# Strassen over the last 192 rows of a down projection as two 96-row halves

## The chip, the cores and the metric

The kernel runs on one core of one Trainium2 chip. The metric is device time in microseconds (us) of that core for one execution. "Span" is the part of it that a profile records; it is about 2 us shorter than the time (254.3 against 256.17 us in the profiled run of the kernel before). I give the ratios with their 95% intervals.

## The reference, cut to what matters

The block is a layer norm with modulation, a spectral filter, a second layer norm with modulation, and a SwiGLU feed-forward part. Only the last part is changed.

```python
# x: (1, 2048, 640), w_gate and w_up: (640, 1728), w_down: (1728, 640), all bf16
h = _layernorm(x, axis=-1) * (1 + cb) + sb
x = x + gb * ((silu(h @ w_gate) * (h @ w_up)) @ w_down)
```

The inner width is 1728 = 12 x 128 + 192. The 192 rows left over are the subject.

## The kernel before

The 2048 tokens are taken in five chunks of 2, 4, 4, 4 and 2 token tiles (128 tokens each). In each chunk TensorE first makes gate and up, and then the down projection. Chunk 0 is done plainly. In chunks 1 to 4 both parts use Strassen's scheme (Winograd's variant) with seven products for eight. In the down projection two token tiles are a "pair"; the halves of the inner width are six blocks of 128 rows each, and the halves of the output are 320 columns. The left-hand sums S1 to S4 are made by VectorE for each pair, the sums T1 to T4 of the weights once. Block 12 (128 rows) and block 13 (64 rows) stay outside the scheme and are multiplied plainly, partly in a folded form (`S12`, `W13`).

```python
def down_pair(ATc, t, j, nxt):                     # a pair of token tiles
    X, Y, Z = (psum[:, next_banks(1), 0:320] for _ in range(3))
    ...
    mm(Z, r13[0:64], Wd_sb[0:64, 13, 0:320], True)           # two 64-row matmuls
    mm(Y, r13[64:128], Wd_sb[64:128, 13, 320:640], True)
    prod(X, A11, B11, True, True)
    nc.scalar.copy(cps_[0], X)
    nc.gpsimd.tensor_tensor(xa[:, 0:320], xa[:, 0:320], cps_[0], ALU.add)
    for k in range(3):
        mm(Z, A12[:, k], B21[:, k])
    prod(Y, S1, T1)
    nxt(0)                                         # VectorE: a sum of the next pair
    mm(Y, ATc[:, 12, tb:tb + 128], w12(1), stop=True)
    nc.scalar.copy(cps_[1], Y)
    prod(X, S2, T2, stop=True)
    nxt(1)
    nc.scalar.copy(cps_[2], X)
    nc.gpsimd.tensor_tensor(xb[:, 320:640], xb[:, 320:640], cps_[1], ALU.add)
    prod(Y, S4, B22)
    nxt(3)
    nc.gpsimd.tensor_tensor(xa[:, 320:640], xa[:, 320:640], cps_[2], ALU.add)
    prod(X, S3, T3, stop=True)
    nc.scalar.copy(cps_[3], X)
    nxt(2)
    ...                                            # blocks 12 and 13, the rest of Z
    prod(X, A22, T4, stop=True)                    # accumulates on the same bank X
    out_store(t, Z, 0)                             # VectorE adds x1, then a store
    out_store(t + 1, X, 0)
```

Gate and up of block 13 share one matmul. Its result lies with gate in partitions 0 to 63 and up in 64 to 127, so it is brought together by four evacuations and two transfers:

```python
def gu13(ci, ATc):
    ...
    nc.scalar.activation(m13[0:64], gv[0:64, 1], ACT.Silu)
    nc.vector.tensor_copy(m13[64:128], gv[64:128, 0])
    nc.scalar.activation(f13[0:64], gv[0:64, 0], ACT.Silu)
    nc.vector.tensor_copy(f13[64:128], gv[64:128, 1])
    nc.sync.dma_start(b13[0:64], m13[64:128])
    nc.sync.dma_start(b13[64:128], m13[0:64])
```

Between gate/up and the pairs of chunk 1 stand the statistics of the second layer norm for token tiles 10 to 15:

```python
if ci == 1:
    ln2_var(10, 6)        # VectorE, 3 small operations
    ln2_pow(10, 6)        # GpSimd, the power -1/2
    ln2_nb(10, 6)         # VectorE, the bias -mean * rstd
...
g21b, g22b = (rL.cut(1024 * i, [512]) for i in range(2))      # gate activations, bytes 0 to 2048 of rL
cps_ = [rL.cut((2560, 10496, 0, 1280)[i], [320], F32) for i in range(4)]   # cps_[2] is at byte 0 of rL
```

## Time and profile before

The median was 256.27 us (256.12 to 256.96, 3 runs). The span of the profile is 254.3 us.

The profile page of the kernel before, first lines: busy time of each engine with its share of the span, and the granted TensorE clock by slices.

```profile
PE 244.9 (96%) x2520; PEld 199.5 (78%) x2520; DVE 208.0 (82%) x521; ACT 163.7 (64%) x305; POOL 73.6 (29%) x117
...
PEclk9999999999999999999999999999999999999999
```

PE is TensorE, DVE VectorE, ACT ScalarE, POOL GpSimd. TensorE is busy for 96% at the full clock. VectorE with 82% is next, and I take it for a likely second limit wherever its work is bunched.

The view of waits of TensorE, kernel before, from 85 to 250 us (engine, tile, line, what it waited for, then total, number, longest):

```profile
PE psum L933 <- DVE rX L1037: 0.8, 1, 0.8
PE psum L1058 <- ACT rH L1090: 0.2, 1, 0.2
```

So in the whole feed-forward part TensorE waited about 1 us. The longer of the two waits is in the last pair. The timeline of TensorE shows it, and shows the start of a pair of chunk 1 (start, duration, engine, line, operation, tiles, shape, count, and in brackets the idle time before):

```profile
134.03 0.27 PE L1058 MATMUL psum<-rW,rH 128*128 128x256 bf16 x1
134.24 1.64 PE L933 MATMUL psum<-rA,rX 64*128 64x320 bf16 x11
...
246.42 0.31 PE L933 MATMUL psum<-rA,rX 128*128 128x320 bf16 x1 [0.78 <-DVE rX L1037]
```

The starts of the single matmuls show what the grouped line hides. The first 64-row matmul starts 205 ns after the last gate/up matmul, where 109 are usual there. The second starts 4 ns after the first. The next full one starts 239 ns later, then comes 146, then 136 ns each. The trace records the two as 64*128, the matmuls around them as 128*128. Together the starts are about 0.2 us a pair longer than the usual ones (205 less 109, 4 + 239 less 136, and 146 less 136). "Drain" is my name for this extra time; the trace doesn't show what TensorE does in it.

### The profile page before, as it was taken

The numbers are of one execution on the slowest core, as the hardware profiler recorded it, in microseconds if no ns is written. First come the engines' busy times: TensorE is split into PE (matmuls) and PEld (weight loads), VectorE is DVE, ScalarE is ACT, GpSimd is POOL, SyncE is SP. The second block draws the span as 40 slices with busy tenths as digits, with TensorE's granted clock in tenths as the row PEclk, the third lists the DMA queues.
The fourth block names the chain that finished last, engine by engine and source line by source line (L and its number), as shares of the span: only waits on it lengthen the run. The fifth ranks groups of instructions, "written<-read, shape, count | busy, mean of one in ns | idle before, by whom it ended". The sixth has DMA issues, their size and how long they took to land.

```text
span 254.3 us, 6501 instructions
## 1 busy us (share of the span) xinstructions
PE 244.9 (96%) x2520; PEld 199.5 (78%) x2520; DVE 208.0 (82%) x521; ACT 163.7 (64%) x305; POOL 73.6 (29%) x117
## 2 busy tenths in 40 slices
PE   8899987999999999999999999999999999999984
PEld 3788856999788887788877678886668886679953
DVE  2898888888888897979997995879985788994793
ACT  3778656988778698578863477673356766235730
POOL 4387756764021805000004600001430000440021
PEclk9999999999999999999999999999999999999999
DMA  7989999999999899710005120002411000212001
GB/s 222 389 278 336 306 394 190 270 275 390 309 332 281 221 257 156 153 36 0 3 0 106 39 70 8 3 3 52 92 40 35 3 0 4 52 52 59 4 0 52
DMA packets 46588, 34.78 MB, mean 137 GB/s; under 512 B 22111, under 2 KB 43486, under 8 KB 46174
## 3 DMA queue, kind: packets, MB, share of 16 engines
q1 hardware_dynamic: 44892, 30.36, 43.2%
q0 software_dynamic: 1376, 3.93, 6.6%
q8 instruction: 19, 0.31, 0.5%
q10 hardware_dynamic: 290, 0.08, 0.1%
q14 instruction: 11, 0.09, 0.1%
HBM read 26.80 MB, written 4.72 MB: 124 GB/s over the span
## 4 chain that ended last, share of the span: by engine, by line
PE 69%; DVE 5%; ACT 4%; DMA 3%; SPq 2%; issue 1%; DVEq 0%; ACTq 0%
PE psum L1058 29%; PE psum L933 17%; PE psum L1031 8%; DMA rM<-in_w_mod_dram 3%; PE psum L645 3%; SPq L504 2%; PE psum L803 2%; PE psum L580 2%; PE psum L806 2%; PE psum L912 1%; PE psum L551 1%; DVE rA L898 1%; PE psum L601 1%; PE psum L1010 1%; PE psum L650 1%
## 5 line engine op out<-in xcount | busy, mean ns | idle before, releaser
L1058 PEld LDWEIGHTS <-rW 128*128 128x128 bf16 (+1 forms) x528 | 47.0, 98 | 5.9 <-issue 0.6
L949 POOL TENSOR_TENSOR rM<-rM,rL 128x320 f32<-128x320 f32 x7 | 6.2, 885 | 86.4 <-ACT rL L948 86.4
L1058 PE MATMUL psum<-rE,rW 128*128 128x256 f16 (+1 forms) x192 | 27.7, 259 | 0.2 <-ACT rH L1090 0.2
L1058 PE MATMUL psum<-rW 128*128 128x256 bf16 (+1 forms) x240 | 27.1, 259 | 0.0
L1058 PE MATMUL psum<-rY,rW 128*128 128x256 bf16 (+1 forms) x96 | 24.0, 259 | 0.0
L573 DVE TENSOR_TENSOR rM<-psum,rW 128x384 bf16<-128x384 f32 (+2 forms) x42 | 20.4, 542 | 3.7 <-PE psum L551 3.4
L933 PEld LDWEIGHTS <-rX 128*128 128x128 bf16 (+1 forms) x181 | 16.1, 97 | 9.2 <-issue 1.6
L1031 PE MATMUL psum<-rW 128*128 128x256 bf16 (+1 forms) x170 | 23.2, 291 | 0.0
L933 PEld LDWEIGHTS <-rE 128*128 128x128 f16 x168 | 16.4, 98 | 6.5 <-DVE rE L884 0.2
L933 PE MATMUL psum<-rE 128*128 128x320 f16 x126 | 20.4, 299 | 0.0
L933 PE MATMUL psum<-rA,rX 128*128 128x320 bf16 (+1 forms) x119 | 19.5, 301 | 0.8 <-DVE rX L1037 0.8
L1031 PEld LDWEIGHTS <-rW 128*128 128x128 bf16 x170 | 16.6, 98 | 3.8
L1058 PEld LDWEIGHTS <-rE 128*128 128x128 f16 x192 | 17.4, 98 | 2.3
L1108 DVE TENSOR_TENSOR rX<-rH,rL 128x512 bf16<-128x512 bf16 x21 | 8.9, 425 | 11.7 <-ACT rL L1106 11.5
L736 POOL TENSOR_TENSOR rstd<-rstd,mhalf 128x4 f32<-128x4 f32 (+2 forms) x4 | 4.7, 1187 | 44.8 <-DVE rstd L732 44.8
L1098 DVE TENSOR_TENSOR rX<-psum,rX 128x512 f32<-128x512 f32 x21 | 14.4, 688 | 3.2 <-ACT rX L1097 2.9
L1097 ACT COPY rX<-psum 128x512 f32<-128x512 f32 x21 | 12.3, 587 | 7.2 <-PE psum L1058 7.1
L1094 DVE TENSOR_TENSOR rH<-psum,rW 128x512 bf16<-128x512 f32 x21 | 14.5, 690 | 2.4 <-PE psum L1058 0.6
L1090 ACT COPY rH<-psum 128x512 f32<-128x512 f32 x21 | 12.2, 581 | 6.4 <-PE psum L1058 5.7
L1084 ACT COPY rW<-psum 128x512 f32<-128x512 f32 x21 | 12.3, 586 | 5.8 <-PE psum L1058 5.8
L390 DVE SCALAR_TENSOR_TENSOR rE<-rE,mv,psum 128x648 bf16<-128x648 f32 (+1 forms) x17 | 14.1, 841 | 2.0 <-PE psum L323 1.6
L1058 PE MATMUL psum<-rW,rE 128*128 128x256 bf16 (+1 forms) x96 | 15.1, 259 | 0.0
(203 smaller groups left out, 665.5 us busy)
## 6 DMA issues: line engine op xcount, KB each, us to landing
out_dram<-rA SPq DMA_DIRECT2D x31, 80.0 KB, 1.6
rM<-in_w_mod_dram SPq DMA_DIRECT2D x3, 800.0 KB, 9.2
rA<-in_B_w_down_dram SPq DMA_DIRECT2D x1, 2080.0 KB, 12.8
rX<-in_A_x_dram SPq DMA_DIRECT2D x3, 640.0 KB, 7.2
rM<-in_w_mod_dram SPq DMA_DIRECT2D x1, 1600.0 KB, 8.0
rY<-in_B_w_gate_dram POOLq DMA_DIRECT2D x2, 768.0 KB, 6.9
rW<-in_B_w_gate_dram SPq DMA_DIRECT2D x2, 640.0 KB, 7.0
rW<-in_B_w_up_dram SPq DMA_DIRECT2D x2, 640.0 KB, 8.0
```

Of the source, the lines that this page charges most:

```text
L390: nc.vector.scalar_tensor_tensor(Zv[:, h], Cv[:, h], mv[:, t, 0:1], zps[:, h], ALU.mult, ALU.subtract)
L573: nc.vector.tensor_tensor(PP[:, :, hl], xv[:, :, hl], in1, ALU.mult)
L645: nc.tensor.matmul(vps[:, r, :], lhsT=Em[:, v, 4 * t + r, :], rhs=Htab[:, t, v, :], start=(v == 0), stop=(v == 1))
L933: nc.tensor.matmul(o, lhsT=lhsT, rhs=rhs, start=start, stop=stop, skip_group_check=True)
L1031: nc.tensor.matmul(gu[u], lhsT=Wgu[:, u, c5, ff * 128:(ff + 1) * 128], rhs=h2T[:, :, c5, :], start=(c5 == 0), stop=(c5 == NC5 - 1))
L1058: nc.tensor.matmul(o[:, f], lhsT=w, rhs=b, start=(start and f == 0 and i == 0), stop=(stop and f == F - 1 and i == len(ops) - 1), skip_gro ...
L1084: nc.scalar.copy(c0, X)
L1090: nc.scalar.copy(c2, X)
L1094: nc.vector.tensor_tensor(c11, Z, c0, ALU.add)
L1097: nc.scalar.copy(c3, X)
L1098: nc.vector.tensor_tensor(c22, Y, c3, ALU.add)
L1108: nc.vector.tensor_tensor(ato, v4(c11), v4(g21), ALU.mult)
```

## The change

The intent is to take the last 192 rows into Strassen's scheme. They become two halves of 96 rows, so that each of the seven products has seven matmuls, the last of 96 rows, and nothing is left outside. Blocks 12 and 13 are stored as rows 1536 to 1632 and (in another order) 1632 to 1728. The transfers between partitions go: VectorE multiplies the up half in partitions 64 to 127 by the activated gate half in partitions 0 to 63. A fourth PSUM bank W takes the last product, so bank X is added to the input by GpSimd, as the fourth addition of a pair.

```diff
-        mm(Z, r13[0:64], Wd_sb[0:64, 13, 0:320], True)
-        mm(Y, r13[64:128], Wd_sb[64:128, 13, 320:640], True)
-        prod(X, A11, B11, True, True)
+        W = psum[:, next_banks(1), 0:320]
+        last = t + 2 == NT
+        prod(X, half(0, ta), wd(0, 0), True, True)       # half(), s7(): 6 x 128 rows and 96 rows
 ...
-        prod(X, S3, T3, stop=True)
-        nc.scalar.copy(cps_[3], X)
+        prod(X, s7(2), t7(2), stop=True)
 ...
+            nc.scalar.copy(cps_[3], X)
+            nc.gpsimd.tensor_tensor(xb[:, 0:320], xb[:, 0:320], cps_[3], ALU.add)
+            out_store(t + 1, cps_[3], 1)
+            prod(W, half(1, tb), t7(3), True, True)
+            out_store(t + 1, W, 0)
 ...  # gate and up of the 64-row block
-        nc.sync.dma_start(b13[0:64], m13[64:128])
-        nc.sync.dma_start(b13[64:128], m13[0:64])
+        nc.scalar.activation(sg13, g13[0:64], ACT.Silu)
+        return lambda: nc.vector.tensor_tensor(ATc[0:64, 13, :], g13[64:128], sg13, ALU.mult)
 ...  # block 12 of gate and up: 96 rows, and 32 rows that go to block 13
+                    nc.vector.tensor_tensor(ATc[0:RK, 12, :], gu[1][0:RK], sg[0:RK, 0:N], ALU.mult)
+        half.rest = lambda: nc.vector.tensor_tensor(ATc[64:RK, 13, :], gu[1][RK:P], sg[RK:P, 0:N], ALU.mult)
 ...  # VectorE order at the end of gate/up of a chunk of four tiles
-            run(2)
-            step(5, nG - 1)
-            step(7, nG - 1)
+            later[:0] = [half.rest, q1, q2]               # q1 to q4: the 96-row sums of the first pair
+            later.extend([q3, q4, lambda: step(8, nG - 1), lambda: step(7, nG - 1)])
+            step(5, nG - 1, True)
 ...  # in the first pair: sums of the second
-                    if n == 4:
+                    if n == 4 and i < 4:
                         a_sum(ATc, 1, i)
+                        a_sum7(ATc, 1, i)
```

The full diff holds more moves: the product Z runs in one piece, the last pair gets its own order, block 13 of chunk 0 moves in front of the last spectral tile, and some squares of the second layer norm come earlier.

The rest product and the four 96-row sums of the first pair now stand before the statistics of chunk 1 in VectorE's order, and the last product of the group (`step(7)`) now comes after them.

More of the change, by code (lines that the diff above doesn't have):

```diff
@@ L29 @@
 IDLE = (3, 6, 1, 2)
+RK = 96
 _NPBF = ml_dtypes.bfloat16
@@ L698, in adaln_block_kernel @@
         nc.vector.tensor_tensor(RI[:, 0], RI[:, 0], ga_bc[:], ALU.mult)
-    nc.sync.dma_start(Wd_sb[:, 0:13, :], B_w_down[0:1664, :].rearrange("(fc fp) d -> fp fc d", fp=P))
-    for h in range(2):
-        nc.sync.dma_start(Wd_sb[64 * h:64 * h + 64, 13, :], B_w_down[1664:1728, :])
+    nc.sync.dma_start(Wd_sb[:, 0:12, :], B_w_down[0:1536, :].rearrange("(fc fp) d -> fp fc d", fp=P))
+    nc.sync.dma_start(Wd_sb[0:RK, 12, :], B_w_down[1536:1632, :])
+    nc.sync.dma_start(Wd_sb[0:64, 13, :], B_w_down[1664:1728, :])
+    nc.sync.dma_start(Wd_sb[64:RK, 13, :], B_w_down[1632:1664, :])
     Wgu = rW.cut(0, [2, NC5, 13 * 128])
@@ L790, in wd_fold @@
     def wd_fold(f2):
-        nc.vector.tensor_tensor(Wd_sb[:, f2, :], Wd_sb[:, f2, :], gb_bc[:], ALU.mult)
-    if True:
-        VTs = {0: s1er(0), 1: s1er(1)}
-        nc.vector.tensor_copy(gb_bc[:, 0:320], mod_bc(3, 0, 7))
-        for t in range(NT):
-            if t and t + 1 < NT:
-                s1em(t + 1)
-                VTs[t + 1] = s1er(t + 1)
-            VT = VTs.pop(t)
-            ops = banks(6 * (t % 2), 2, [4, 256])[:, :, 0:160]
-            for h in range(2):
-                nc.tensor.matmul(ops[:, 2 * h:2 * h + 2], lhsT=VT[:, 4, :], rhs=RI[:, 1, 2 * h:2 * h + 2, :],
-                                 start=True, stop=False)
-                for rr in range(2):
-                    nc.tensor.matmul(ops[:, 2 * h + rr], lhsT=VT[:, 2 * h + rr, :], rhs=RI[:, 0, 2 * h + rr, :],
-                                     start=False, stop=(rr == 1))
-            nc.vector.scalar_tensor_tensor(x1[:, t, :].rearrange("p (m r) -> p m r", r=4), ops.rearrange("p r m -> p m r"), 1.0,
-                                           x_sb[:, t, :].rearrange("p (m r) -> p m r", r=4), ALU.mult, ALU.add,
-                                           accum_out=st2[:, t, 0:1])
-            if t in (8, 11):
-                gu_dma(GS[0][:], B_w_gate, t // 11 * 2, 2, t == 8)
-            if 1 <= t <= 2:
-                ln2_sq(t - 1)
-            if t == 3:
-                ln2_var(0, 2)
-                ln2_pow(0, 2)
-            if 4 <= t <= 5:
-                ln2_xn(0, t - 4)
-            if t == 5:
-                ln2_tr(0)
-                load_gu(1024, 1664)
-            if t in (7, 9, 11, 13):
-                ln2_sq(2 + (t - 7) // 2)
-            if t == 10:
-                ln2_mod(0)
-            if t == 14:
-                ln2_var(2, 4)
-                ln2_pow(2, 4)
-            if t >= 7 and t % 2:
-                wd_fold((13, 0, 1, 2, 3)[(t - 7) // 2])
-        for o, n, r, w in ((GS[2], 2, 0, B_w_gate), (UG.unsqueeze(1), 1, 4, B_w_gate), (GS[2], 2, 0, B_w_up), (UG.unsqueeze(1), 1, 4, B_w_up)):
-            gu_dma(o[:], w, r, n, w is B_w_gate)
+        rows = slice(0, P if f2 < 12 else RK)
+        nc.vector.tensor_tensor(Wd_sb[rows, f2, :], Wd_sb[rows, f2, :], gb_bc[rows], ALU.mult)
     ring = [2]
@@ L847, in adaln_block_kernel @@
     Hs = [rE.cut(21504 + 1024 * i, [2, 256], F16) for i in range(4)]
-    S12 = rY.cut(6144, [128], F16)
+    T7 = [rE.cut(37888 + 640 * i, [320], F16, parts=RK) for i in range(4)]
+    S7 = [rH.cut(256 * i, [128], F16, parts=RK) for i in range(4)]
     nh = rY.cut(6400, [4, 128])
-    W13 = rH.cut(0, [2, 320])
     tmp = [r.cut(off, [512], F32) for r, off in ((rW, 45056), (rW, 47104), (rH, 4352), (rH, 6400))]
@@ L872, in wd_rest, with sums, a_sum, a_sum7 @@
     def wd_rest():
-        nc.vector.memset(W13[0:64, 0], 0.0)
-        nc.vector.tensor_copy(W13[64:128, 0], Wd_sb[64:128, 13, 0:320])
-        nc.vector.tensor_copy(W13[0:64, 1], Wd_sb[0:64, 13, 320:640])
-        nc.vector.tensor_scalar_mul(W13[64:128, 1], Wd_sb[64:128, 13, 320:640], -1.0)
-    def a_sum(ATc, j, i, ks=slice(0, 6)):
-        a11, a12, a21, a22 = (ATc[:, HK * f + ks.start:HK * f + ks.stop, 256 * j + 128 * h:256 * j + 128 * h + 128]
-                              for h in range(2) for f in range(2))
-        s1, s2, s3, s4 = (x[:, ks] for x in (S1, S2, S3, S4))
+        b11, b12 = (Wd_sb[0:RK, 12, 320 * h:320 * h + 320] for h in range(2))
+        b21, b22 = (Wd_sb[0:RK, 13, 320 * h:320 * h + 320] for h in range(2))
+        tt = nc.vector.tensor_tensor
+        tt(T7[0], b12, b11, ALU.subtract)
+        tt(T7[1], b22, T7[0], ALU.subtract)
+        tt(T7[2], b22, b12, ALU.subtract)
+        tt(T7[3], b21, T7[1], ALU.subtract)
+    def sums(i, s, a11, a12, a21, a22):
         tt = nc.vector.tensor_tensor
         if i == 0:
-            tt(s1, a21, a22, ALU.add)
+            tt(s[0], a21, a22, ALU.add)
         elif i == 1:
-            tt(s2, s1, a11, ALU.subtract)
+            tt(s[1], s[0], a11, ALU.subtract)
         elif i == 2:
-            tt(s3, a11, a21, ALU.subtract)
-        elif i == 3:
-            tt(s4, a12, s2, ALU.subtract)
-        else:
-            tt(S12, ATc[:, 12, 256 * j:256 * j + 128], ATc[:, 12, 256 * j + 128:256 * j + 256], ALU.subtract)
+            tt(s[2], a11, a21, ALU.subtract)
+        else:
+            tt(s[3], a12, s[1], ALU.subtract)
+    def a_sum(ATc, j, i, ks=slice(0, 6)):
+        sums(i, [x[:, ks] for x in (S1, S2, S3, S4)],
+             *(ATc[:, HK * f + ks.start:HK * f + ks.stop, 256 * j + 128 * h:256 * j + 128 * h + 128]
+               for h in range(2) for f in range(2)))
+    def a_sum7(ATc, j, i):
+        sums(i, S7, *(ATc[0:RK, 12 + f, 256 * j + 128 * h:256 * j + 128 * h + 128] for h in range(2) for f in range(2)))
     def out_store(t, src, h, o=0, n=320):
@@ L902, in down_plain @@
         for tl in range(n):
-            if tl % 2 == 0:
-                pops = [[psum[:, next_banks(1), 0:320] for _ in range(2)] for _ in range(2)]
-                for h in range(2):
-                    for s in range(2):
-                        rows = slice(64 * s, 64 * s + 64)
-                        nc.tensor.matmul(pops[s][h], lhsT=ATc[rows, 13, 64 * tl:64 * tl + 128],
-                                         rhs=Wd_sb[rows, 13, 320 * h:320 * h + 320], start=True, stop=False)
-            for h in range(2):
-                for fc in range(NFC - 1):
-                    nc.tensor.matmul(pops[tl % 2][h], lhsT=ATc[:, fc, tl * 128:(tl + 1) * 128],
-                                     rhs=Wd_sb[:, fc, 320 * h:320 * h + 320], start=False, stop=(fc == NFC - 2))
-                out_store(t0 + tl, pops[tl % 2][h], h)
+            for h in range(2):
+                pop = psum[:, next_banks(1), 0:320]
+                for fc in range(NFC):
+                    rows = slice(0, P if fc < 12 else RK)
+                    nc.tensor.matmul(pop, lhsT=ATc[rows, fc, tl * 128:(tl + 1) * 128],
+                                     rhs=Wd_sb[rows, fc, 320 * h:320 * h + 320], start=(fc == 0), stop=(fc == NFC - 1))
+                out_store(t0 + tl, pop, h)
                 if tl == h == 0:
@@ L933, in mm, with half, wd, s7 @@
             nc.tensor.matmul(o, lhsT=lhsT, rhs=rhs, start=start, stop=stop, skip_group_check=True)
-        def prod(o, lhs, rhs, start=False, stop=False):
-            for k in range(HK):
-                mm(o, lhs[:, k], rhs[:, k], start and k == 0, stop and k == HK - 1)
-        def w12(h):
-            return Wd_sb[:, 12, 320 * h:320 * h + 320]
-        A11, A12 = ATc[:, 0:HK, ta:ta + 128], ATc[:, HK:2 * HK, ta:ta + 128]
-        A22 = ATc[:, HK:2 * HK, tb:tb + 128]
-        r13 = ATc[:, 13, 128 * j:128 * j + 128]
-        mm(Z, r13[0:64], Wd_sb[0:64, 13, 0:320], True)
-        mm(Y, r13[64:128], Wd_sb[64:128, 13, 320:640], True)
-        prod(X, A11, B11, True, True)
+        def half(f, o):
+            return [ATc[:, HK * f + k, o:o + 128] for k in range(HK)] + [ATc[0:RK, 12 + f, o:o + 128]]
+        def wd(f, h):
+            return [Wd_sb[:, HK * f + k, 320 * h:320 * h + 320] for k in range(HK)] + [Wd_sb[0:RK, 12 + f, 320 * h:320 * h + 320]]
+        def s7(i):
+            return [(S1, S2, S3, S4)[i][:, k] for k in range(HK)] + [S7[i]]
+        def t7(i):
+            return [(T1, T2, T3, T4)[i][:, k] for k in range(HK)] + [T7[i]]
+        def prod(o, lhs, rhs, start=False, stop=False, ks=range(HK + 1)):
+            for k in ks:
+                mm(o, lhs[k], rhs[k], start and k == 0, stop and k == HK)
+        W = psum[:, next_banks(1), 0:320]
+        last = t + 2 == NT
+        prod(X, half(0, ta), wd(0, 0), True, True)
         nc.scalar.copy(cps_[0], X)
         nc.gpsimd.tensor_tensor(xa[:, 0:320], xa[:, 0:320], cps_[0], ALU.add)
-        for k in range(3):
-            mm(Z, A12[:, k], B21[:, k])
-        prod(Y, S1, T1)
+        prod(Z, half(1, ta), wd(1, 0), True, ks=range(0, HK))
+        if last:
+            prod(W, half(1, tb), t7(3), True, ks=range(0, 2))
+        prod(Y, s7(0), t7(0), True, True)
         nxt(0)
-        mm(Y, ATc[:, 12, tb:tb + 128], w12(1), stop=True)
         nc.scalar.copy(cps_[1], Y)
-        prod(X, S2, T2, stop=True)
+        prod(Z, half(1, ta), wd(1, 0), stop=True, ks=(HK,))
+        prod(X, s7(1), t7(1), stop=True)
         nxt(1)
@@ L959, in down_pair @@
         nc.gpsimd.tensor_tensor(xb[:, 320:640], xb[:, 320:640], cps_[1], ALU.add)
-        prod(Y, S4, B22)
+        out_store(t, Z, 0)
+        prod(Y, s7(3), wd(1, 1), stop=True)
         nxt(3)
         nc.gpsimd.tensor_tensor(xa[:, 320:640], xa[:, 320:640], cps_[2], ALU.add)
-        prod(X, S3, T3, stop=True)
-        nc.scalar.copy(cps_[3], X)
+        prod(X, s7(2), t7(2), stop=True)
         nxt(2)
-        mm(Y, S12, w12(1))
         nxt(4)
-        mm(Y, r13, W13[:, 1], stop=True)
         out_store(t, Y, 1)
-        for k in range(3, HK):
-            mm(Z, A12[:, k], B21[:, k])
-        mm(Z, ATc[:, 12, ta:ta + 128], w12(0), stop=True)
-        out_store(t + 1, cps_[3], 1)
-        mm(X, ATc[:, 12, tb:tb + 128], w12(0))
-        mm(X, r13, W13[:, 0])
-        if t + 2 < NT:
-            prod(X, A22, T4, stop=True)
-            out_store(t, Z, 0)
-            out_store(t + 1, X, 0)
-        else:
-            out_store(t, Z, 0)
+        if not last:
+            nc.scalar.copy(cps_[3], X)
[3 more added lines that the diff above has]
+            out_store(t + 1, W, 0)
+        else:
+            nc.vector.tensor_tensor(xb[:, 0:320], X, xb[:, 0:320], ALU.add)
+            out_store(t + 1, X, 1)
             for lo in (0, 160):
-                prod(X[:, lo:lo + 160], A22, T4[:, :, lo:lo + 160], stop=True)
+                prod(W[:, lo:lo + 160], half(1, tb), [w[:, lo:lo + 160] for w in t7(3)], stop=True, ks=range(2, HK + 1))
             for lo in (0, 160):
-                out_store(t + 1, X[:, lo:lo + 160], 0, lo, 160)
+                out_store(t + 1, W[:, lo:lo + 160], 0, lo, 160)
     def h_parts(ci):
@@ L1010, in gu13 @@
             nc.tensor.matmul(g13, lhsT=Wp13[:, c5, :], rhs=h2T[:, :, c5, :], start=(c5 == 0), stop=(c5 == NC5 - 1))
-        gv = g13.rearrange("p (j s q) -> p s j q", s=2, q=128)
-        f13 = rX.cut(14336, [n // 2, 128], F32)
-        m13 = rX.cut(14336 + 1024, [n // 2, 128])
-        b13 = rX.cut(14336 + 1536, [n // 2, 128])
-        nc.scalar.activation(m13[0:64], gv[0:64, 1], ACT.Silu)
-        nc.vector.tensor_copy(m13[64:128], gv[64:128, 0])
-        nc.scalar.activation(f13[0:64], gv[0:64, 0], ACT.Silu)
-        nc.vector.tensor_copy(f13[64:128], gv[64:128, 1])
-        nc.sync.dma_start(b13[0:64], m13[64:128])
-        nc.sync.dma_start(b13[64:128], m13[0:64])
-        return lambda: nc.vector.tensor_tensor(ATc[:, 13, 0:64 * n], f13[:].rearrange("p j q -> p (j q)"),
-                                               b13[:].rearrange("p j q -> p (j q)"), ALU.mult)
+        sg13 = rX.cut(14336, [512], F32, parts=64)[:, 0:128 * n]
+        nc.scalar.activation(sg13, g13[0:64], ACT.Silu)
+        return lambda: nc.vector.tensor_tensor(ATc[0:64, 13, :], g13[64:128], sg13, ALU.mult)
     def gu_plain(ci, ATc, ff, sg):
@@ L1036, in half @@
                 between()
-                nc.vector.tensor_tensor(ATc[:, ff, :], gu[1], sg[:, 0:N], ALU.mult)
+                if ff < 12:
+                    nc.vector.tensor_tensor(ATc[:, ff, :], gu[1], sg[:, 0:N], ALU.mult)
+                else:
+                    nc.vector.tensor_tensor(ATc[0:RK, 12, :], gu[1][0:RK], sg[0:RK, 0:N], ALU.mult)
+        half.rest = lambda: nc.vector.tensor_tensor(ATc[64:RK, 13, :], gu[1][RK:P], sg[RK:P, 0:N], ALU.mult)
         return half
@@ L1068, in bank, with step @@
             return v(psum[:, next_banks(1), :])
-        def step(i, g):
+        def step(i, g, sep=False):
             if not 0 <= g < nG:
@@ L1100, in step @@
                 mms(Y, g, [(GS[3], b22), (UG, hb)], False, True)
+                if sep:
+                    return
+                nc.vector.tensor_tensor(c12, Y, c2, ALU.add)
+            elif i == 8:
                 nc.vector.tensor_tensor(c12, Y, c2, ALU.add)
@@ L1151, in gate_up_pairs @@
         step(6, nG - 1)
+        q1, q2, q3, q4 = (lambda q=q: a_sum7(ATc, 0, q) for q in range(4))
         if n == 2:
-            step(5, nG - 1)
+            step(5, nG - 1, True)
+            half(1)
+            step(8, nG - 1)
             step(7, nG - 1)
@@ L1156, in gate_up_pairs @@
             r1, r2, r3, r4 = (lambda q=q: a_sum(ATc, 0, q, slice(2, 6)) for q in range(4))
-            later[:] = [r1, r2, s4, r4, s3, r3]
-            half(1, lambda: run(2))
+            later[:] = [r1, half.rest, q1, r2, q2, s4, r4, q4, s3, r3, q3]
         else:
@@ L1161, in gate_up_pairs, with at_of @@
             half(1, lambda: run(len(later) - 2))
-            run(2)
-            step(5, nG - 1)
-            step(7, nG - 1)
+            later[:0] = [half.rest, q1, q2]
+            later.extend([q3, q4, lambda: step(8, nG - 1), lambda: step(7, nG - 1)])
+            step(5, nG - 1, True)
         run(len(later))
-        a_sum(ATc, 0, 4)
+    def at_of(ci):
+        N = 128 * chunks[ci][1]
+        return AT[:, 0:NFC * N].rearrange("p (f q) -> p f q", f=NFC)
+    if True:
+        VTs = {0: s1er(0), 1: s1er(1)}
+        nc.vector.tensor_copy(gb_bc[:, 0:320], mod_bc(3, 0, 7))
+        for t in range(NT):
+            if t and t + 1 < NT:
+                s1em(t + 1)
+                VTs[t + 1] = s1er(t + 1)
+            VT = VTs.pop(t)
+            if t == NT - 1:
+                fin13 = gu13(0, at_of(0))
+            ops = banks(6 * (t % 2), 2, [4, 256])[:, :, 0:160]
+            for h in range(2):
+                nc.tensor.matmul(ops[:, 2 * h:2 * h + 2], lhsT=VT[:, 4, :], rhs=RI[:, 1, 2 * h:2 * h + 2, :],
+                                 start=True, stop=False)
+                for rr in range(2):
+                    nc.tensor.matmul(ops[:, 2 * h + rr], lhsT=VT[:, 2 * h + rr, :], rhs=RI[:, 0, 2 * h + rr, :],
+                                     start=False, stop=(rr == 1))
+            nc.vector.scalar_tensor_tensor(x1[:, t, :].rearrange("p (m r) -> p m r", r=4), ops.rearrange("p r m -> p m r"), 1.0,
+                                           x_sb[:, t, :].rearrange("p (m r) -> p m r", r=4), ALU.mult, ALU.add,
+                                           accum_out=st2[:, t, 0:1])
+            if t in (8, 11):
+                gu_dma(GS[0][:], B_w_gate, t // 11 * 2, 2, t == 8)
+            if 1 <= t <= 2:
+                ln2_sq(t - 1)
+            if t == 3:
+                ln2_var(0, 2)
+                ln2_pow(0, 2)
+            if 4 <= t <= 5:
+                ln2_xn(0, t - 4)
+            if t == 5:
+                ln2_tr(0)
+                load_gu(1024, 1664)
+            if t in (5,7,9,11):
+                ln2_sq(2 + (5,7,9,11).index(t))
+            if t == 10:
+                ln2_mod(0)
+            if t == 14:
+                ln2_var(2, 4)
+                ln2_pow(2, 4)
+            if t >= 7 and t % 2:
+                wd_fold((13, 0, 1, 2, 3)[(t - 7) // 2])
+        for o, n, r, w in ((GS[2], 2, 0, B_w_gate), (UG.unsqueeze(1), 1, 4, B_w_gate), (GS[2], 2, 0, B_w_up), (UG.unsqueeze(1), 1, 4, B_w_up)):
+            gu_dma(o[:], w, r, n, w is B_w_gate)
@@ L1168, in adaln_block_kernel @@
     for ci, (t0, n) in enumerate(chunks):
         N = 128 * n
-        ATc = AT[:, 0:NFC * N].rearrange("p (f q) -> p f q", f=NFC)
+        ATc = at_of(ci)
         if ci:
@@ L1173, in adaln_block_kernel @@
         else:
-            fin13 = gu13(ci, ATc)
             for fc in range(NFC - 1):
@@ L1179, in adaln_block_kernel @@
                 half(1)
-                if fc == 10:
+                if fc == 12:
+                    half.rest()
+                if fc == 0:
                     fin13()
-                if fc == 0:
                     ln2_nb(2, 4)
```

## The prediction

> **What bounds it now.** TensorE. The timeline of the matmuls from 85 us to 243 us has no hole above 0.2 us; only the end has one (1.0 us between issues, 245.4 to 246.4, waiting for the VectorE product of row block 12). So the change pays by what it takes from the TensorE stream and from that end, and costs where VectorE becomes late.
>
> **Removed.** Per pair of token tiles there are 50 matmuls of 320 columns. 48 start 136 ns apart. The two 64-row ones start together (4 ns), but the first starts 205 ns after its predecessor (109 expected), the next full one 239 ns later, then 146: about 0.21 us of drain. [...] Afterwards there are 7 products of 7 matmuls: 49 slots instead of 48 and one shared. So Strassen on the last rows saves only the drain: 7 x 0.21 = 1.5 us, if 96 rows run without a switch. The plain chunk goes the other way: 56 slots (7.62 us) against 52, two shared ones and drains (7.54): +0.07. The ping-pong of ScalarE (0.38 us) and VectorE (0.43 us) evacuations and two transfers for the 64-row block at each chunk start goes; the waits behind it at 111.0 and 151.9 are worth 0.25 us. Block 13 of chunk 0 moves into a 0.4 us hole at 84.2, but its input is ready only at 84.54 (GpSimd), so 0.1 us.
>
> **Added.** VectorE: per pair four 96x128 sums (0.2 us each, as the 128x128 ones) for one; per chunk one 32-row product (0.6 us). GpSimd: a fourth 0.9 to 1.2 us addition per pair; while it runs, VectorE additions take 1.0 instead of 0.4 us.
>
> **Where this reaches TensorE.** In the two pairs of a full chunk VectorE is already busy nearly without a break (134 to 150, 175 to 190). Its modulation and sums of the next chunk's input come last. In chunk 1 the modulation ends at 147.1, and the 64-row gate/up block uses it at 148.3: slack 1.2, minus 0.4 because TensorE arrives earlier. I expect VectorE 1.5 to 2 us later there (products, sums, then the GpSimd power that it waits for), so a new hole near 1 us at the start of chunk 2. In chunk 2 the slack is 2 us: hole 0 to 0.5. In chunk 3 none.
>
> **The end.** The 1.0 us hole shrinks since the block-12 product comes first, but VectorE gets about 1.5 us more in a tail that had 1.6 us of idle: gain 0.3, plus or minus 0.5 (without the drain).
>
> **Sum.** -1.5 + 0.07 - 0.25 - 0.1 - 0.3 + 1.0 + 0.2 = -0.9 us. Predicted 255.3 us, 8 in 10 between 254.1 and 256.7. Faster by over 2%: 2%. Within 2%: 97%. Slower by over 2%: 1%.
>
> **What would show it.** Matmul starts in the pairs 136 ns apart, a pair in 6.66 instead of 6.87 us: right on the drain. A gap near 240 ns around the 96-row ones: wrong, they switch too. A TensorE wait for VectorE at the start of chunk 2 (about 147 to 150): right on lateness; none: the sums were hidden, and the time is nearer 254.2. In the last 8 us: VectorE with no idle left and products waiting for the sums.
>
> **What would make it wrong.** 96-row matmuls that switch mode (over 1 us a pair); VectorE much later than estimated, in every chunk; a tail bound by GpSimd alternating with VectorE; block 13 of chunk 0 stalling TensorE behind a later input.

The sum: the seven come to -0.88, given as -0.9 us (with 7 x 0.21 = 1.47 unrounded, as in the table further down, -0.85). "Drain" and "switch" stand for the longer starts around the matmuls that the trace records as 64*128, about 0.21 us a pair, and for nothing else that was shown. "1.0 instead of 0.4 us" can be read from a 128x512 sum with both operands in SBUF (L996, kernel before): 1.08 us beside a GpSimd addition at 185.27, 0.41 without one at 147.06. The 0.6 us of the 32-row product was an estimate; it took 0.69 in the kernel after (L996 there, 32x512).

## More of the kernel before

L743 is the bias of the statistics; L884, L886 and L890 are the sums S1, S2 and S4 of the second pair:

```profile
138.50 0.82 DVE L743 SCALAR_TENSOR_TENSOR nb<-st,rstd 128x6 f32<-128x6 f32 x1 [1.45 <-POOL rstd L736]
139.25 0.54 DVE L884 TENSOR_TENSOR rE<-rX 128x768 f16<-128x768 bf16 x1
139.90 1.03 DVE L886 TENSOR_TENSOR rE<-rE,rX 128x768 f16<-128x768 f16 x1
141.03 1.03 DVE L890 TENSOR_TENSOR rE<-rX,rE 128x768 f16<-128x768 bf16 x1
```

VectorE stands still for 1.45 us in the middle of its busiest stretch, waiting for the GpSimd power. S4 is nevertheless ready at 141.03 + 1.03 = 142.06, and the second pair multiplies it from 144.34 (timeline of TensorE): 2.3 us of slack.

## The result, and the profile after

The kernel after took 259.63 us median (258.43 to 260.01, 4 runs), the ratio to the kernel before is 1.0116 [1.0077, 1.0154]. A ratio is the mean time of one kernel's runs over that of the other's of the same rounds, so not quite the ratio of the medians that I quote. Executions over 1.5% slower than the fastest of the same kernel are left out of the means. A repetition gave 259.06 us (258.57 to 260.44, 6 runs) against 256.92 (255.68 to 257.80, 11 runs), ratio 1.0089 [1.0057, 1.0121]. So the change costs about 1%. The sign of my prediction was wrong, and both medians lie outside its range.

The page of the kernel after:

```profile
PE 245.4 (95%) x2512; PEld 201.0 (78%) x2512; DVE 214.8 (83%) x538; ACT 163.1 (63%) x299; POOL 79.2 (31%) x123
...
PEclk9799999999999999999999999999999999999998
```

TensorE is about as busy as before, VectorE has 6.8 us more and GpSimd 5.6 us more. The 7 in the second slice of the clock is one window of 3.4 us at half rate near the start (a clock record of 3413 ns at 0.5, from 7.63 to 11.04 us). The page of the repetition shows no such slice, but only because its first clock record is at 10.86 us: until then its matmuls run as slowly (the one at 7.80 us is followed by the next after 0.26 us, where the kernel before took 0.13 for the same two). So the half rate came twice with this kernel. Six of the ten profiles of kernels with the change don't have it, so the change doesn't bring it each time; neither of the two profiles without the change has it, so whether it is chance alone stays open.

The waits of TensorE in the kernel after, from 85 to 250 us, say where the time went:

```profile
PE psum L1017 <- DVE rE L963: 1.0, 1, 1.0
PE psum L894 <- DVE rE L848: 0.8, 1, 0.8
PE psum L894 <- DVE rE L850: 0.8, 1, 0.8
PE psum L894 <- ACT rL L926: 0.4, 2, 0.2
PE psum L894 <- DVE rE L844: 0.4, 1, 0.4
PE psum L973 <- POOL rW L764: 0.3, 1, 0.3
```

L850 and L848 make the sums S4 and S3, L963 makes the last sum of the next chunk's input, L926 is ScalarE's copy into `cps_[2]`, and L844 makes S1 of the last pair. L973 is block 13 of chunk 0, which waits for its input from GpSimd (L764); my prediction had named this as a risk. To weigh them I cut both traces into stages, from the first matmul of one to the first of the next (worked out from the recorded starts; "pairs" is two pairs):

| stage, us | before | after | difference |
|---|---|---|---|
| last spectral tile to gate/up of chunk 0 | 2.76 | 2.61 | -0.15 |
| gate/up and plain down, chunk 0 | 14.29 + 7.45 | 14.19 + 7.62 | +0.07 |
| gate/up, chunk 1 | 27.14 | 26.82 | -0.32 |
| **pairs, chunk 1** | 13.64 | 15.37 | **+1.73** |
| **gate/up, chunk 2** | 27.25 | 28.09 | **+0.84** |
| pairs, chunk 2 | 13.64 | 13.74 | +0.10 |
| gate/up, chunk 3 | 26.91 | 26.82 | -0.09 |
| pairs, chunk 3 | 13.64 | 13.74 | +0.10 |
| gate/up, chunk 4 | 13.79 | 13.70 | -0.09 |
| last pair to the end of the span | 11.17 | 11.55 | +0.38 |
| sum | 171.68 | 174.25 | +2.57 |

(The sum leaves out what comes before the last spectral tile.) Against the repetition the same table gives the same values within 0.03 us in all but the first row. The front part, up to the last spectral stage, was 65.1 us before and 66.5 after. Over the twelve profiles it falls into groups: 66.1 to 66.5 us in the four where TensorE ran at half rate until about 11 us (the kernel after, its repetition, and the runs with early statistics and with `cps_[2]` moved), 65.6 and 66.2 us in two where TensorE waited 1.1 and 1.7 us near 53 us for a transfer from `w_mod` (the better tail and both mends), and 64.6 to 65.1 us in the other six. It follows these two events and not the edits, four kernels with the change being in the last group, so I do not count it. What is left, +2.6 us, is 1.0% and agrees with the two ratios, though the timed runs may also hold some of the half rate.

The timeline of TensorE in the kernel after, in the pairs of chunk 1 and at the start of chunk 2:

```profile
137.01 0.98 PE L894 MATMUL psum<-rE 128*128 128x320 f16 x6
137.83 0.30 PE L894 MATMUL psum<-rE,rH 96*128 96x320 f16 x1
137.97 0.30 PE L894 MATMUL psum<-rA,rX 96*128 96x320 bf16 x1
...
146.71 0.99 PE L894 MATMUL psum<-rA,rE 128*128 128x320 bf16 x6 [0.81 <-DVE rE L850]
148.67 0.99 PE L894 MATMUL psum<-rE 128*128 128x320 f16 x6 [0.83 <-DVE rE L848]
...
153.95 0.61 PE L1017 MATMUL psum<-rE 128*128 128x256 f16 x4 [1.03 <-DVE rE L963]
```

The first three lines show that the 96-row matmuls run like full ones: they start 0.14 us apart (the starts around them are 135 to 140 ns apart, where 136 is usual), without the gap of 239 ns and without the 4 ns between the two 64-row ones. The drain is gone, although the trace records them as 96*128. The last three lines are the new holes: two in the second pair of chunk 1, one at the start of chunk 2.

VectorE in that stretch, kernel after (L844, L846, L850, L848 are S1, S2, S4, S3; "96x128" are the new sums):

```profile
141.08 0.83 DVE L745 SCALAR_TENSOR_TENSOR nb<-st,rstd 128x6 f32<-128x6 f32 x1 [1.44 <-POOL rstd L738]
141.83 1.29 DVE L844 TENSOR_TENSOR rE<-rX 128x768 f16<-128x768 bf16 x1
143.04 0.88 DVE L844 TENSOR_TENSOR rH<-rX 96x128 f16<-96x128 bf16 x1
143.84 0.54 DVE L846 TENSOR_TENSOR rE<-rE,rX 128x768 f16<-128x768 f16 x1
144.31 0.88 DVE L846 TENSOR_TENSOR rH<-rH,rX 96x128 f16<-96x128 f16 x1
145.11 0.48 DVE L864 TENSOR_TENSOR rA<-psum,rM 128x320 bf16<-128x320 f32 x1
145.51 1.14 DVE L850 TENSOR_TENSOR rE<-rX,rE 128x768 f16<-128x768 bf16 x1
```

and GpSimd beside it:

```profile
139.72 1.33 POOL L738 TENSOR_TENSOR rstd<-rstd,mhalf 128x6 f32<-128x6 f32 x1 [38.43 <-ACT rL L926]
141.03 0.85 POOL L916 TENSOR_TENSOR rM<-rM,rL 128x320 f32<-128x320 f32 x1
141.85 0.85 POOL L927 TENSOR_TENSOR rM<-rM,rL 128x320 f32<-128x320 f32 x1
142.66 1.17 POOL L931 TENSOR_TENSOR rM<-rM,rL 128x320 f32<-128x320 f32 x1
143.80 1.31 POOL L938 TENSOR_TENSOR rM<-rM,rL 128x320 f32<-128x320 f32 x1
```

The bias comes 5.86 us after the start of the pairs (141.08 less 135.22), where it came 4.26 after it before (138.50 less 134.24). (The bracket of the power names a ScalarE copy, which ended at 139.68. What the power needs is VectorE's L734, the last of the three operations on statistics, which ended at 139.63; the power starts 0.08 us after it, as it started 0.08 us after L732 before.) From then on GpSimd has its additions back to back, because they had queued behind the power (the ScalarE copies for the first three ended at 136.82, 138.59 and 139.68), and most of VectorE's sums, which read both operands from SBUF, take longer beside them: a 96x128 sum of 0.22 us elsewhere takes 0.88, and three of the four 768-wide ones (0.54 alone) take 1.14 to 1.29. The addition with one operand in PSUM (L864) keeps its 0.48 beside the GpSimd addition that starts at 145.07. S4 is ready at 146.65, which is 11.43 us after the start of the pairs instead of 7.82, so 3.6 us later: 1.6 of it from the later bias, 2.0 from the longer row of sums.

The loss was thus about as large for a small sum (0.66 us) as for a large one (0.60 to 0.75): in this stretch it went by the number of instructions and not by their size. The GpSimd additions also grew, from 0.85 to 1.17 and 1.31 us. The trace shows these durations and not their cause; that it goes by where the operands lie is my inference from the sums and L864.

The second new wait is smaller. In chunks 2 and 3 (ScalarE and TensorE, timeline of the kernel after):

```profile
183.36 0.42 ACT L926 COPY rL<-psum 128x320 f32<-128x320 f32 x1 [1.31 <-DVE rX L1066]
183.84 0.97 PE L894 MATMUL psum<-rE 128*128 128x320 f16 x6 [0.20 <-ACT rL L926]
```

L1066 is `step(7)`, the product that reads `g22b`. `cps_[2]` lies over `g21b` and part of `g22b`, so the copy of bank X must wait for it (1.31 us), and the next product into X waits for the copy (0.20 us).

### The profile page after: what moved, and what is told of

Read it like the earlier page. It is cut to its first block, busy times and chain, and to the rows that moved or that the text cites. A ratio compares the mean times of both kernels' runs of the same rounds, so it can differ in the third digit from the quotient of the medians.

```text
span 258.2 us, 6489 instructions
## 1 busy us (share of the span) xinstructions
PE 245.4 (95%) x2512; PEld 201.0 (78%) x2512; DVE 214.8 (83%) x538; ACT 163.1 (63%) x299; POOL 79.2 (31%) x123
## 5 line engine op out<-in xcount | busy, mean ns | idle before, releaser
L894 PEld LDWEIGHTS <-rX 128*128 128x128 bf16 (+1 forms) x152 | 14.4, 97 | 5.7 <-DVE rX L994 0.5
L894 PE MATMUL psum<-rA,rX 128*128 128x320 bf16 (+1 forms) x98 | 15.7, 299 | 0.0
L344 ACT COPY rE<-psum 128x640 bf16<-128x640 bf16 x16 | 11.1, 692 | 7.1 <-PE psum L342 7.1
```

The lines of the kernel that those rows point to most:

```text
L344: nc.scalar.copy(hT[:, :, 0:128], _rev(xt, 127, [[128, NC5], [-1, 128]]) if flipped(t) else xt)
L894: nc.tensor.matmul(o, lhsT=lhsT, rhs=rhs, start=start, stop=stop, skip_group_check=True)
```

## The experiments

**Theories.** A: the statistics of chunk 1, pushed back by the rest product and the 96-row sums, make VectorE late and bunch GpSimd's additions; the late sums S4 and S3 stop TensorE. B (rival): the work itself is too much, so the fourth GpSimd addition, or the 96-row sums, would stop TensorE wherever they stand. C: the copy into `cps_[2]` waits because its memory is still read. D: the fourth bank and its addition are to blame, and three banks would do better. Stage values below are in the order of the table above; the kernels of one paragraph were timed beside the kernel before on the same chip.

**Repetition of the kernel after**, unchanged.

> The changed kernel itself, unaltered. The profiled run had a window of 3.4 us at half clock at 7.8 us, which cost 1.6 us, and the four times ran from 258.4 to 260.0. If that window is chance, the profile here has a granted clock of 1.0 and about 258.4 us (2.1 us over before), and the spread is found again; if it belongs to the change, it is in this profile too, and in no profile of before.

Measured: 259.06 us, ratio 1.0089 [1.0057, 1.0121], as told above. Pairs of chunk 1 again 15.37 us, gate/up of chunk 2 again 28.09. The stages are reproducible; the total is not so to better than about 1 us. The expectation that the profile would come without the half rate, at about 258.4 us, was wrong: the half rate was there again until 10.86 us, and the profiled run took 260.08. Its 1.6 us for the window was an estimate; the front part was 1.4 us longer (66.5 against 65.1).

**Statistics early (theory A against B).** The three operations on statistics move from before the pairs of chunk 1 into its gate/up part, where GpSimd is idle (38.43 us before the power in the kernel after).

```diff
-        if ci == 1:
-            ln2_var(10, 6)
-            ln2_pow(10, 6)
-            ln2_nb(10, 6)
+    def early_stats(i):                  # called from the extra work of gate/up, chunk 1
+        if i == 0:
+            ln2_var(10, 6)
+            ln2_pow(10, 6)
+        elif i == 1:
+            ln2_nb(10, 6)
```

> One part moved: the variance, GpSimd power and bias of the last six tiles, which stand between the sums of chunk 1 and those of its second pair, are issued in the gate/up stage of chunk 1. Theory A (the extra products and sums stand in front of a serial wait of 2.3 us there, so everything after it is late): the two waits of 1.0 us in the second pair of chunk 1 and the 1.2 us at the start of chunk 2 go, 2.5 to 3.1 us faster than the changed kernel. Rival B (VectorE lacks throughput because the fourth GpSimd addition blocks it): most of these waits stay, under 0.8 us faster.

Measured: 257.37 us (255.84 to 259.85; one of the six runs, the longest, is not in the ratio), ratio 0.9993 [0.9957, 1.0028]. The pairs of chunk 1 went from 15.37 to 13.76 us and the gate/up part of chunk 2 from 28.09 to 26.82, so 2.88 us came back (by the ratios about 2.5, against 1.0089 of the repetition), and the waits for L850, L848 and L963 are gone from the view of waits. GpSimd and VectorE of this kernel in the pairs of chunk 1:

```profile
137.11 0.86 POOL L916 TENSOR_TENSOR rM<-rM,rL 128x320 f32<-128x320 f32 x1 [20.63 <-ACT rL L915]
138.81 0.86 POOL L927 TENSOR_TENSOR rM<-rM,rL 128x320 f32<-128x320 f32 x1 [0.84 <-ACT rL L922]
...
140.08 0.56 DVE L844 TENSOR_TENSOR rE<-rX 128x768 f16<-128x768 bf16 x1
140.55 0.21 DVE L844 TENSOR_TENSOR rH<-rX 96x128 f16<-96x128 bf16 x1
```

GpSimd now waits for the copies, so its additions have gaps (0.84 us here), and most 96x128 sums fall into gaps and take 0.21 again. The same sums and the same four additions, moved by nothing but an earlier power, no longer stop TensorE there. Theory A holds. B as "too much work wherever it stands" falls for these waits.

**`cps_[2]` moved (theory C).**

```diff
-    cps_ = [rL.cut((2560, 10496, 0, 1280)[i], [320], F32) for i in range(4)]
+    cps_ = [rL.cut((2560, 10496, 9216, 1280)[i], [320], F32) for i in range(4)]
```

> One address changed: the ScalarE copy of the third partial product no longer lies on the gate activations that the last product of a chunk still reads. Theory: the copy waits for that product since the change moved the product behind the sums; the 0.37 us waits in the first pair of chunks 2 and 3 go, 0.5 to 0.9 us faster in all. Rival (the wait is a late VectorE sum): no change, within 0.2 us.

Measured: 257.81 us (257.69 to 259.64), ratio 1.0049 [1.0016, 1.0082], next to 1.0089 of the kernel after. The pairs of chunks 2 and 3 take 13.38 us each, 0.36 less. The copy now waits only for its product:

```profile
182.49 0.43 ACT L926 COPY rL<-psum 128x320 f32<-128x320 f32 x1 [0.66 <-PE psum L894]
```

In chunk 1 the pairs gained 0.33 us too (15.04), and the start of chunk 2 gave 0.20 back (28.29): as long as VectorE is late there, an earlier TensorE only waits longer. C is shown.

**Three banks instead of four (theory D).** Bank W goes; bank X is copied after the S3 product and the last product is accumulated on it, as before; the fourth GpSimd addition goes.

```diff
-        W = psum[:, next_banks(1), 0:320]
 ...
+        nc.scalar.copy(cps_[3], X)
 ...
-            nc.gpsimd.tensor_tensor(xb[:, 0:320], xb[:, 0:320], cps_[3], ALU.add)
-            prod(W, half(1, tb), t7(3), True, True)
+            prod(X, half(1, tb), t7(3), stop=True)
```

> The fourth PSUM bank per pair undone, and with it the fourth GpSimd addition; the last product is added onto the third in PSUM as before, and the order of the Z product is that of before; the 96-row sums stay. Theory A: VectorE gains 0.5 to 0.7 us per pair in chunk 1, 0.8 to 1.5 us faster than the changed kernel, the wait at the start of chunk 2 shrinks but some stays. Rival B (the fourth addition is the cause): 2.5 us faster or more, no waits of the second pair for its sums.

Measured: 259.96 us (259.36 to 260.82), ratio 1.0120 [1.0089, 1.0150]. The run is confounded. Chunk 1 became better (pairs 13.94, gate/up of chunk 2 27.41), but the pairs of chunks 2 and 3 became worse (15.19 each), because with this order of products the copy into `cps_[2]` is due earlier and its memory is still read:

```profile
180.40 0.43 ACT L922 COPY rL<-psum 128x320 f32<-128x320 f32 x1 [2.36 <-DVE rX L1061]
180.88 0.97 PE L894 MATMUL psum<-rE 128*128 128x320 f16 x6 [1.39 <-ACT rL L922]
```

It shows cause C a second time, four times as large, and says nothing about D by itself. The fair comparison comes last.

**Both mends on the kernel after**: statistics early and `cps_[2]` moved.

> Both mends of before (early statistics, moved copy) in the changed kernel. If the two causes are separate, chunk 1's pairs take 13.4 us (15.37 in the changed kernel), the gate/up stage of chunk 2 26.8 (28.1), the pairs of chunks 2 and 3 13.4 each (13.74): 4.0 us less than the changed kernel from the last spectral stage on, 1.2 us less than before, about 255.2 us. If one hides the other, less than 3.3 us.

Measured: 255.16 us (254.12 to 256.16, 6 runs) against 256.36 (255.82 to 257.13, 11 runs), ratio 0.9951 [0.9925, 0.9977]. All three stages of two pairs take 13.38 us, the gate/up parts of chunks 1 to 3 take 26.82 each. TensorE's waits from 85 to 250 us:

```profile
PE psum L973 <- POOL rW L764: 0.4, 1, 0.4
PE psum L894 <- DVE rE L844: 0.4, 1, 0.4
```

The stages of the table sum to 170.46 us, 1.22 less than before; the ratio says 0.49% of 256.4, so 1.25. Not all of that is the change's: the next run, the kernel before with early statistics, has a sum of 171.42, so against it the change with both mends is worth 0.96 us. Its two side effects cost 3.8 us (174.25 less 170.46), about four times as much.

**The kernel before with early statistics** (control): the same move in the kernel without the change.

> The same early statistics in the kernel before the change, as a control. Theory: TensorE waited there only 0.34 us at the start of chunk 2, so at most that is gained, and the stages are otherwise the same to 0.05 us. Rival (the statistics cost as much in both, and the move is a gain by itself): 1 us or more.

Measured: 255.85 us (255.24 to 256.83), ratio 0.9982 [0.9957, 1.0007]. Only gate/up of chunk 2 changed, from 27.25 to 26.99 us. So the power was an almost harmless wait before, and early statistics alone do not make the kernel of the last paragraph: 0.96 of its 1.22 us come from the change and the mends together. The intervals of the two ratios overlap, so it is the stages that separate the kernels, not the times.

**No fourth addition** (wrong result on purpose, relative error 0.029; one look): tells which part of the work made VectorE late in theory A.

```diff
-            nc.gpsimd.tensor_tensor(xb[:, 0:320], xb[:, 0:320], cps_[3], ALU.add)
```

> Wrong result on purpose: the fourth GpSimd addition of a pair is left out, all else as in the changed kernel. Theory A': the additions do not cause the lateness, but in chunk 1 they prolong it, since there GpSimd runs without a break from 141 to 148 us beside the sums: chunk 1's pairs and chunk 2's start lose 1 to 2 of the 3.0 us that they are longer, the stages of chunks 2 and 3 do not change (under 0.1 us). Rival B: all waits in the pairs go, in chunks 2 and 3 too.

Measured: pairs of chunk 1 14.63 us (0.74 less than after), gate/up of chunk 2 27.48 (0.61 less), with waits of 0.8 for L848 and of 0.5 at the start of chunk 2 left. So the fourth addition carries about half of the 2.88 us, but only beside the late statistics: in chunks 2 and 3 taking it away changed nothing (13.75 and 13.74).

**No 96-row sums** (wrong result on purpose, relative error 0.024; one look): the 96-row matmuls read the raw rows instead.

```diff
-        sums(i, S7, *(ATc[0:RK, 12 + f, ...] for h in range(2) for f in range(2)))
+        pass
 ...
-            return [...] + [S7[i]]
+            return [...] + [ATc[0:RK, 12 + i % 2, ta:ta + 128]]
```

> Wrong result on purpose: the changed kernel without the 96-row sums on VectorE; the products read rows of the activations in their place, so TensorE has the same work. Theory A: four of these sums stand in front of the statistics of chunk 1 (about 0.9 us) and four among the sums of the second pair, so the bias ends about 0.9 us earlier after the start of the pairs, and chunk 1's pairs with chunk 2's start lose 1.5 to 2.5 of their 3.0 us. Rival C (the moved products alone, not the sums, make it late): under 0.7 us of it goes.

Measured: pairs of chunk 1 13.38 us (1.99 less), gate/up of chunk 2 27.63 (0.46 less). The bias came 5.20 us after the start of the pairs instead of 5.86, so 0.66 earlier, where I expected 0.9. So the sums carry most of it. The last pair to the end took 11.03 us here instead of 11.56, less than the 11.17 before. The two parts are not additive: 1.35 for the addition and 2.45 for the sums make 3.8 us, more than the 2.88 that early statistics alone give back. Each keeps the other from fitting.

**A better tail** on the kernel with both mends: in the last pair the W product goes before the second Y product, the S3 product comes last in two halves, and the last stores are spread over two queues.

```diff
+            prod(W, half(1, tb), t7(3), stop=True, ks=range(2, HK + 1))
+            nc.vector.tensor_tensor(xb[:, 0:320], W, xb[:, 0:320], ALU.add)
         prod(Y, s7(3), wd(1, 1), stop=True)
 ...
+                    (nc.scalar if h else nc.sync).dma_start(out_v[...], xl[h][...])
```

> Early statistics and moved copy, and the last pair in another order: the product that needs no sum runs before the second use of Y, its addition is done while TensorE goes on, and the third product onto X comes last, in two halves. Theory (the end is bound by the sums on VectorE at first and by five VectorE operations after the third product at the last): from the first product of the last pair to the last VectorE operation 8.0 us instead of 8.7, 0.5 to 0.8 us faster than the kernel with the two mends alone. Rival (the end hangs on GpSimd's additions): no gain.

Measured: 255.28 us (254.25 to 255.66), ratio 0.9948 [0.9926, 0.9970]. The stage from the last pair to the end went from 11.56 us (kernel with both mends) to 11.32. The total does not resolve that: 255.28 against 255.16. Its last four additions of VectorE come after the last matmul:

```profile
249.65 1.02 DVE L952 TENSOR_TENSOR rA<-psum,rM 128x160 bf16<-128x160 f32 x4 [0.28 <-PE psum L894]
```

The stores are quicker (2.63 against 2.92 us from the end of VectorE to the end of the span), the additions are not: from the first product of the last pair to VectorE's end it took 8.7 us, where I expected 8.0 (8.6 with both mends alone).

**Three banks with both mends** (theory D, fair).

> Three banks per pair instead of four, as in the run with three banks, but with early statistics and the moved copy, against the kernel with these two mends and four banks. If the fourth bank is worth what it saves on TensorE (the wait of 0.13 us per pair for ScalarE's copy of X), this one is slower by 0.8 us in all or more, with the pairs of a chunk at 13.6 us against 13.38. If the fourth addition on GpSimd costs more than that, it is faster.

Measured: 256.69 us (255.26 to 256.80) against 256.40 (255.48 to 257.67), ratio 1.0006 [0.9976, 1.0036]. The two pairs take 13.64 us instead of 13.38 in each of the three chunks, and the last pair to the end takes 11.98 instead of 11.56. 13.64 is also what the kernel before took, so without the fourth bank no gain from the drain would be left inside the pairs. So the fourth bank is worth 0.13 us a pair to TensorE, and D falls: once the two mends are in, the kernel with four banks is better by 1.2 us in these stages (3 x 0.26 + 0.42), about 0.5%. The ratios, 0.9951 and 1.0006, say the same, but come from two chips.

## Why the prediction was right or wrong

The table sets the terms of the prediction against the stages. "Drain" in the first row is for the six pairs of chunks 1 to 3, and is read where no wait hides it, in the kernel with both mends.

| term, us | predicted | measured |
|---|---|---|
| drain, six pairs | -1.26 (6 x 0.21) | -1.05 |
| last pair and end, with its drain | -0.51 | +0.29 |
| ping-pong at the starts of chunks 1 and 2 | -0.25 | -0.57 |
| chunk 0, plain | +0.07 | +0.07 |
| block 13 of chunk 0 | -0.1 | -0.15, not resolved (a wait of 0.3 is in it) |
| hole at the start of chunk 2 | +1.0 | +1.27 |
| hole at the start of chunk 3 | +0.2 | 0 |
| sums of the second pair, chunk 1 | not seen | +1.61 |
| `cps_[2]`, chunks 1 to 3 | not seen | +1.10 |
| sum | -0.85 | +2.57 |

How the measured column is made: the drain is 3 x (13.64 less 13.38) + 3 x 0.09 at the entries (26.91 less 26.82). The last pair is 11.55 less 11.17, less the 0.09 of its entry. The ping-pong is 27.14 less 26.82 and 27.25 less 26.82, each less 0.09. The hole of chunk 2 is 28.09 less 26.82. The unseen terms are 15.37 less 13.76 (what early statistics gave back in these pairs), and 13.76 less 13.38 (chunk 1, with early statistics) + 2 x (13.74 less 13.38). The first row of stages was 2.20 us in the two profiles without the wait in block 13 of chunk 0, and 2.61 to 2.86 in the eight others with the change.

**What was right.** The 96-row matmuls show no drain (135 to 140 ns between starts) and a pair without waits takes 6.69 us, near the 6.66 that I gave. The plain chunk costs what I worked out. The hole at the start of chunk 2 came, with about the size I gave (1.27 us between the stages, 1.03 of it in the named wait), and none came in chunk 3. Late VectorE was named as the danger.

**The step that failed** is the paragraph "Where this reaches TensorE". It says that the modulation and sums of the next chunk's input "come last", and it looks for slack only there: 1.2 us at the start of chunk 2. VectorE's work for the second pair of the same chunk comes sooner, and I did not ask when that was due. It had 2.3 us of slack for S4 in the trace before. I also put the lateness of the modulation at 1.5 to 2 us; counted from the start of the pairs it ended 3.4 us later (16.34 against 12.91), and S4 3.6 us later. The prediction names the power, and that additions are slowed beside GpSimd, but not how the two join, which the trace before already shows: VectorE stands still behind the power (1.45 us), so all that is put ahead of it delays the power, and GpSimd's additions queue behind the power and then run back to back (138.45, 139.27 and 140.48 us there), so that in the kernel after a small sum of 0.22 us costs 0.88. Early statistics removed 2.88 us; taking away either half of the new work removed 1.35 or 2.45. This step is the largest, but it doesn't turn the sign alone: without the 1.61 us the sum would be about +1.0, and without the next one as well about -0.1.

**A second step that was missing** is a check of buffers against the new order. I costed instructions, not the memory that they release. `step(7)` was moved behind the new sums, and the copy of bank X into `cps_[2]` over `g22b` then waited 1.31 us. Moving the buffer shows it, at 0.36 us in each of chunks 2 and 3; in chunk 1 it gave 0.33 alone and 0.38 beside early statistics.

**A term with the wrong size and sign** is the end. The 0.78 us wait for block 12 did go, and TensorE started its last matmul 0.40 us sooner in that stage (7.34 against 7.74). But S1 of the last pair now runs beside a GpSimd addition (1.01 us, where the kernel before took 0.42), and the last stores follow one another on one queue (four in 3.14 us, where the kernel before took 1.76; kernel after, timeline of the last pair):

```profile
248.46 1.01 DVE L844 TENSOR_TENSOR rE<-rX 128x512 f16<-128x512 bf16 x1
249.53 0.72 PE L894 MATMUL psum<-rE 128*128 128x320 f16 x4 [0.38 <-DVE rE L844]
252.56 3.14 SPq L865 DMA_DIRECT2D out_dram<-rA  x4
```

VectorE ended 0.47 us later after the start of the last matmul, and the span ended 0.31 later after VectorE. The run without the 96-row sums, which ended this stage 0.53 us sooner, shows that these sums carry more than the whole loss. I had weighed VectorE's idle time in the tail, not what follows TensorE's last matmul.

**A term that only looks too small** is the ping-pong: -0.57 against -0.25. Part of it is not the ping-pong's: the control shows that 0.26 us of the hole at the start of chunk 2 came from the late statistics, in the kernel before too. The rest, -0.31, is near what I gave.

**What stays open.** The front part of the kernel scattered by about 2 us from profile to profile. The traces show with what (half rate until about 11 us, or the wait for `w_mod`), but not whether the change makes either likelier: six of ten profiles with it have one of the two, and none of the two profiles without it has half rate or a wait above 0.5 us. How the 2.88 us divide between the addition and the sums can't be said, since they are not additive.

## What to carry to other kernels

When new work is put into an engine's queue, look up when each later instruction of that engine is first needed, nearest first, and not only the one that is due last; and if it stands ahead of a hand-over to another engine and back (here VectorE, GpSimd, VectorE), move that hand-over to where both engines are idle (2.88 us came back here). When an operation moves later, list the buffers that it reads and who will overwrite them. A change that loses 1% may be a gain of some 0.4% (0.96 us here) with two side effects, and a cut of the trace into stages finds them when the total cannot.
